# Routed experts after a spectral mixing layer: the first expert product turned round, in tiles of 512, 256 and 128 rows

## The chip, the core and the metric

One core of a Trainium2 chip runs the kernel. The metric is the device time of one execution in microseconds (us); the median of three runs of the kernel before is 2474.87 us. The profile is one further look at an execution: its span runs from the first to the last instruction. [...]

## The reference, cut to what matters

```python
# x: (8, 2496, 256), all float32
X = np.fft.rfft(x, axis=1)
y = np.fft.irfft(X * (filt_r + 1j * filt_i)[None], n=2496, axis=1)
x = y.reshape(19968, 256)                       # N = 19968 tokens of D = 256
logits = x @ w_gate                             # E = 8 experts
expert = argmax(logits, 1)
gate = softmax(logits)[range(N), expert]
for e in range(8):                              # F = 1024
    rows = (expert == e)
    out[rows] = gate[rows, None] * (np.maximum(x[rows] @ w1[e], 0) @ w2[e])
```

Every token goes to one expert, and none is dropped, so how many rows an expert has is known only on the chip.

## The kernel before, in words

The kernel has two stages. The **transform** takes the eight batches through four small matrix stages (`stage_a`, `stage_bc`, `stage_d`) that overlap from batch to batch and pass their data through DRAM (`zd`, `ud`, `yd`). After each batch `route` finds each token's expert and gate, and scatters (token, gate) into a `table` in DRAM with 26 indirect DMAs from GpSimd (POOL), L368. Expert e's tokens stand in the table from row e*N on. The order of the instructions in this stage is worked out by a planner from its own estimates of their times. The planner also places the eight 1 MB loads of w1 (L391), which stay on the chip in `w1s`, the eight loads of w2 (L438), and the short VectorE program (L405 to L428) that finds for each tile its expert and its first row in the table.

The **expert stage** treats 163 tiles of 128 rows of one expert each. Its order is written out by hand (L511 to L522). For one tile:

- `gather` (L442): SP reads the tile's first row from `rrow` into a register and loads 128 table rows (`idt`, L445); POOL gathers the tokens' rows of `yd` (`xg`, L453). The first of the table loads waits for all scatters.
- `turn_x` (L458): two TensorE transposes of 128x128 bring x into `xT`, with its 256 columns on the partitions, through one PSUM bank and a copy.
- `hidden` (L468): x is stationary, and w1 streams through. Two PSUM banks of 128 rows x 512 hidden columns take two products each; in float32 every product is issued as two instructions. ScalarE and VectorE apply the relu.
- `turn_h` (L483): eight transposes turn h, four to a bank, with a copy by each of ScalarE and VectorE.
- `result` (L495): eight products of 256 columns with the turned h as the stationary side and w2 streaming; ScalarE applies the gates; POOL scatters the rows into the output (L502).

In one step of the loop the gather of tile i, the transposes of x of tile i-3, the transposes of h of tile i-5, the hidden product of tile i-4 and the result of tile i-5 are issued in this order. Each engine runs its own instructions in order, and SP's loads share one DMA queue.

Of the kernel before, what the change touches and what calls it, by code (L numbers as in the profile page):

```python
# [105 lines left out]
    # of P = X*Fr and Q = X*Fi, with Yr = Pr - Qi and Yi = Pi + Qr  # L106
# [13 lines left out]
def kernel(  # L120
# [18 lines left out]
    NT = (N + E * (P - 1)) // P  # L139
    TR = E * N + (NT - N // P + 1) * P  # L140
# [6 lines left out]
    # Expert e's tokens, in any order, from row e*N on: (token, gate); unused rows hold token N.  # L147
# [4 lines left out]
    w1s = perm.tile([P, E, DH, F], F32, name="w1s")  # L152
# [166 lines left out]
    def route(b, lgr):  # L319
# [33 lines left out]
        # row = e*N + count before this batch + in this batch's earlier t + in this t's earlier q  # L353
# [13 lines left out]
        for t in range(N2):  # L367
# [6 lines left out]
            # Every token has a row of its own: the scatters need no order among themselves.  # L374
# [24 lines left out]
    erow = tt.tile([1, NT], I32, name="erow")  # L399
    rrow = tt.tile([1, NT], I32, name="rrow")  # L400
    c_i = tt.tile([1, E], I32, name="c_i")
    nt = tt.tile([1, E], F32, name="nt")
    end = tt.tile([1, E], F32, name="end")
# [142 lines left out]
```

## Time and profile before

| | |
|---|---|
| time, three runs | 2455.88, 2474.87, 2485.93 us |
| median | 2474.87 us |
| span of the profiled execution | 2287.2 us |
| instructions | 25424 |
| PE busy / weight loads (PEld) | 88% / 57% |
| DVE, ACT, POOL busy | 25%, 18%, 23% |
| mean granted clock | 0.917 |
| moved by DMA | 191.90 MB, mean 84 GB/s |

The profiled execution has no time of its own beside its span; the median lies 187.7 us above the span. PE is TensorE's products and transposes, PEld its weight loads, which can run under products. In the timeline a row may merge several instructions of a kind: the row's start is that of the first, its length goes to the end of the last, and x8 is their number. Rows of the DMA-issuing queues (SPq) show when a transfer was issued and not when it landed. [...]

### The profile page before, as it was taken

What the parts mean: (1) busy time and instruction counts of PE and PEld (TensorE: products, weight loads), DVE (VectorE), ACT (ScalarE), POOL (GpSimd) and SP (SyncE); (2) the same over time, 40 slices, a digit from 0 to 9 for tenths busy, and PEclk for the clock granted to TensorE, in tenths of its full rate; (3) what the DMA queues carried; (4) which work ended last, traced back from release to release, by engine and by line L of the source; (5) the groups of instructions that cost most, each with busy time, mean ns of one, the idle gap of its engine ahead of it and who ended that gap; (6) DMA issues with size and microseconds to landing.
All of it is one profiled execution on the core that took longest, in us unless ns stands there. A gap on an engine that the chain in (4) does not pass through costs nothing. (4 is left out here: it accounts for less than half of the span.)

```text
span 2287.2 us, 25424 instructions
## 1 busy us (share of the span) xinstructions
PE 2006.8 (88%) x8246; PEld 1303.9 (57%) x8246; DVE 562.6 (25%) x911; ACT 417.6 (18%) x750; POOL 519.0 (23%) x550
## 2 busy tenths in 40 slices
PE   0468888888888888099999999999999999999998
PEld 0224444444444446066667776667777667777666
DVE  0122323232323233222222222222222222222221
ACT  0112111111211112012222222222222222222221
POOL 0000122130404042622222222222222222222221
PEclk9898779877977788599999999999999999999999
DMA  8875556563837354611111111111111111111110
GB/s 145 231 222 164 135 155 150 144 158 111 185 113 177 112 128 122 154 32 33 34 36 33 32 33 33 34 36 33 32 33 33 33 35 32 33 33 33 35 34 15
DMA packets 127074, 191.90 MB, mean 84 GB/s; under 512 B 41687, under 2 KB 93603, under 8 KB 126596
## 3 DMA queue, kind: packets, MB, share of 16 engines
q1 hardware_dynamic: 104648, 148.28, 25.9%
q0 software_dynamic: 22304, 42.01, 5.8%
q8 instruction: 75, 1.23, 0.2%
q14 instruction: 47, 0.39, 0.1%
HBM read 104.42 MB, written 84.15 MB: 82 GB/s over the span
## 5 line engine op out<-in xcount | busy, mean ns | idle before, releaser
L475 PE MATMUL hps<-w1s,xT 128*128 x1304 | 589.7, 595 | 1.0 <-DMA idt<-table 0.9
L499 PE MATMUL yps<-w2s,hT 128*128 x2608 | 589.6, 379 | 0.3 <-ACT hT L493 0.3
L499 PEld LDWEIGHTS yps<-w2s,hT 128*128 128x128 f32 x2608 | 495.4, 190 | 137.0 <-issue 77.0
L502 POOL DMA_INDIRECT out_dram<-ys,idt x163 | 165.7, 1016 | 933.4 <-ACT ys L501 933.4
L475 PEld LDWEIGHTS hps<-w1s,xT 128*128 128x128 f32 x1304 | 236.1, 191 | 237.2 <-issue 235.9
L368 POOL DMA_INDIRECT table<-pay,row x208 | 193.1, 928 | 766.5 <-DVE row L365 430.4
L281 PE MATMUL bank<-pq,tcs 104*104 104x512 f32 x352 | 226.6, 778 | 84.1 <-DVE pq L270 84.1
L479 DVE TENSOR_SCALAR h<-hps 128x512 f32<-128x512 f32 x163 | 112.8, 692 | 452.6 <-PE hps L475 452.6
L501 ACT ACTIVATE ys<-yps,idt 128x256 f32<-128x256 f32 x163 | 77.4, 475 | 736.3 <-PE yps L499 736.3
L464 DVE COPY xT<-pt 128x256 f32<-128x256 f32 x163 | 69.2, 425 | 505.7 <-PE pt L462 468.0
L270 DVE TENSOR_TENSOR pq<-bank,ht 104x1024 f32<-104x1024 f32 x96 | 117.6, 1225 | 268.6 <-PE bank L266 253.2
L253 PE MATMUL bank<-xt,tas 96*96 96x512 f32 x208 | 119.3, 706 | 65.5 <-DMA xt<-in_x_dram 65.5
L453 POOL DMA_INDIRECT xg<-yd,idt x163 | 158.2, 971 | 60.2 <-issue 53.0
L489 PE MATMUL pt<-ident,h 128*128 128x128 f32 x1304 | 169.2, 273 | 0.1
L281 PEld LDWEIGHTS bank<-pq,tcs 104*104 104x104 f32 x352 | 63.7, 203 | 176.8 <-DVE pq L270 113.5
L481 ACT ACTIVATE h<-hps 128x512 f32<-128x512 f32 x163 | 97.3, 597 | 317.1 <-PE hps L475 317.1
L266 PE MATMUL bank<-zi,tbs 104*104 104x256 f32 x384 | 133.7, 473 | 22.8 <-DMA zi<-zd 22.8
L282 ACT COPY uo<-bank 104x512 f32<-104x512 f32 x96 | 56.3, 586 | 501.5 <-PE bank L281 395.8
L489 PEld LDWEIGHTS pt<-ident,h 128*128 128x128 f32 x1304 | 147.5, 141 | 0.6 <-DVE h L479 0.4
L491 DVE COPY hT<-pt 128x512 f32<-128x512 f32 x163 | 112.8, 692 | 88.1 <-PE pt L489 88.1
L266 PEld LDWEIGHTS bank<-zi,tbs 104*104 104x104 f32 x384 | 78.9, 218 | 77.8 <-issue 60.8
L253 PEld LDWEIGHTS bank<-xt,tas 96*96 96x96 f32 x208 | 40.5, 198 | 136.0 <-issue 66.2
(76 smaller groups left out, 961.2 us busy)
## 6 DMA issues: line engine op xcount, KB each, us to landing
zi<-zd SPq DMA_DIRECT2D x48, 416.0 KB
ud<-uo SPq DMA_DIRECT2D x48, 416.0 KB
xt<-in_x_dram SPq DMA_DIRECT2D x48, 384.0 KB
zd<-zo SPq DMA_DIRECT2D x48, 384.0 KB
ui<-ud SPq DMA_DIRECT2D x48, 384.0 KB
yd<-yo SPq DMA_DIRECT2D x48, 384.0 KB
w1s<-in_moe_w_dram SPq DMA_DIRECT2D x8, 1024.0 KB
w2s<-in_moe_w_dram SPq DMA_DIRECT2D x8, 1024.0 KB
```

The costliest lines, as they stand in the source:

```text
L253: mm(ps[:N1, :], lhsT=tas, rhs=xt[:, j:j + 2, :], start=True, stop=True)
L266: mm(ps[:K2, i * D:(i + 1) * D], lhsT=tbs[:, p0 + j + i, :], rhs=zi[:, j + i, :], start=True, stop=True)
L270: nc.vector.tensor_mul(pq, z2[:, None].to_broadcast((K2, 2, 2, D)), ht[:, :, p0 + j:p0 + j + 2, :])
L281: mm(ps[:K2, :], lhsT=tcs[:, s, :], rhs=pq[:, s], start=(s == 0), stop=(s == 1))
L368: sc = nc.gpsimd.indirect_dma_start(out=table, out_offset=bass.IndirectOffsetOnAxis(ap=row[:, t:t + 1], axis=0), in_=pay[:, t, :], in_offs ...
L453: nc.gpsimd.indirect_dma_start(out=xg, out_offset=None, in_=yd, in_offset=bass.IndirectOffsetOnAxis(ap=idt[i].bitcast(U32)[:, 0:1], axis=0))
L475: mm(ps, lhsT=xT[:, dh, :], rhs=w1s[:, bass.ds(ev, 1), dh, fh * 512:(fh + 1) * 512], start=(dh == 0), stop=(dh == DH - 1))
L479: nc.vector.tensor_scalar_max(o, ps, 0.0)
L489: nc.tensor.transpose(pt[:, j, :], h[:, (k + j) * P:(k + j + 1) * P], ident)
L491: nc.vector.tensor_copy(hs[i][:, k:k + 4, :], pt)
L499: mm(ps, lhsT=hT[:, ft, :], rhs=w2s[:, bass.ds(ev, 1), ft, :], start=(ft == 0), stop=(ft == FT - 1))
L502: nc.gpsimd.indirect_dma_start(out=out, out_offset=bass.IndirectOffsetOnAxis(ap=idt.pop(i).bitcast(U32)[:, 0:1], axis=0), in_=ys, in_offse ...
```

## The change

w1 is no longer kept on the chip. Each tile copies its expert's w1 (1 MB) into one of four buffers `w1t` by a load on SP's queue. In `hidden` a 128x128 block of w1 is the stationary side and the turned x streams, so that h comes out with its hidden columns on the partitions; `turn_h` is gone. Eight PSUM banks per tile are filled one after the other, each by two products of as many columns as the tile has rows. A tile has 512, 256 or 128 rows: 31 of 512 are taken from the experts' full blocks, then 8 of 256, and then 23 of 128; `tile_map` runs three times to find their experts and rows. A tile of 512 rows has one table load, four gathers, and four results of 128 rows each, with four scatters. The copies out of PSUM go to VectorE and ScalarE in turn. In the hand-written order the w2 loads are issued after tile 0's table load and w1 copy; within a step the order is gather and w1 copy of tile i+3, hidden of tile i, transposes of x of tile i+1, result of tile i-1.

```diff
@@ the rows of a tile, the table's size, w1's buffer @@
-    NT = (N + E * (P - 1)) // P
-    TR = E * N + (NT - N // P + 1) * P
+    TILES, left = [], N
+    for rows in (512, 256):
+        n = (left - E * (rows - 1)) // rows
+        TILES.append((rows, n))
+        left -= rows * n
+    TILES.append((P, (left + E * (P - 1)) // P))
+    TR = E * N + (E + 1) * P
-    w1s = perm.tile([P, E, DH, F], F32, name="w1s")
@@ the experts @@
     run_all(a0)
...
-            nc.sync.dma_start(out=w1s[:, e], in_=moe_w1[e].rearrange("(i p) f -> p i f", p=P))
         run_all(*([stage_bc(b)] if b < B else []), *([stage_a(b + 1)] if b + 1 < B else []),
...
     tt = ctx.enter_context(tc.tile_pool(name="tt", bufs=1))
...
+    done = tt.tile([1, E], F32, name="done")
+    nc.vector.memset(done, 0.0)
...
+    def tile_map(rows, n, last):
+        av_i = tt.tile([1, E], I32, name="av_i")
+        av = tt.tile([1, E], F32, name="av")
+        end = tt.tile([1, E], F32, name="end")
+        nc.vector.tensor_tensor(av, cnt[0:1, :], done, op=ALU.subtract)
+        nc.vector.tensor_scalar(av_i, in0=av, scalar1=float(rows - 1 if last else 0), scalar2=None, op0=ALU.add)
+        nc.vector.tensor_scalar(
+            av_i, in0=av_i, scalar1=rows.bit_length() - 1, scalar2=None, op0=ALU.arith_shift_right
+        )
+        nc.vector.tensor_copy(av, av_i)
+        nc.vector.tensor_tensor_scan(end, one, av, 0.0, op0=ALU.mult, op1=ALU.add)
+        base = tt.tile([1, E], F32, name="base")
+        add = tt.tile([1, E], F32, name="add")
+        nc.vector.tensor_tensor(base, done, eoff[0:1, :], op=ALU.add)
+        nc.vector.tensor_scalar(add, in0=av, scalar1=-float(rows), scalar2=None, op0=ALU.mult)
+        nc.vector.tensor_tensor(add, add, base, op=ALU.subtract)
+        nc.vector.tensor_tensor(add[:, :E - 1], add[:, :E - 1], base[:, 1:], op=ALU.add)
+        tau_i = tt.tile([1, n], I32, name="tau_i")
+        tau = tt.tile([1, n], F32, name="tau")
+        nc.gpsimd.iota(tau_i, pattern=[[1, n]], base=0, channel_multiplier=0)
+        nc.vector.tensor_copy(tau, tau_i)
+        past = tt.tile([1, n, E - 1], F32, name="past")
+        she = (1, n, E - 1)
+        nc.vector.tensor_tensor(
+            past, tau[:, :, None].to_broadcast(she), end[:, None, :E - 1].to_broadcast(she), op=ALU.is_ge
+        )
+        ef = tt.tile([1, n], F32, name="ef")
+        erow = tt.tile([1, n], I32, tag=f"erow{rows}", name="erow")
+        nc.vector.tensor_reduce(ef, past, axis=AX.X, op=ALU.add)
+        nc.vector.tensor_copy(erow, ef)
+        nc.vector.tensor_tensor(past, past, add[:, None, :E - 1].to_broadcast(she), op=ALU.mult)
+        rf = tt.tile([1, n], F32, name="rf")
+        rrow = tt.tile([1, n], I32, tag=f"rrow{rows}", name="rrow")
+        nc.vector.tensor_reduce(rf, past, axis=AX.X, op=ALU.add)
+        nc.vector.tensor_scalar(tau, in0=tau, scalar1=float(rows), scalar2=base[:, 0:1], op0=ALU.mult, op1=ALU.add)
+        nc.vector.tensor_tensor(rrow, rf, tau, op=ALU.add)
+        if not last:
+            take = tt.tile([1, E], F32, name="take")
+            nc.vector.tensor_tensor(take, av, end, op=ALU.subtract)
+            nc.vector.tensor_scalar(take, in0=take, scalar1=float(n), scalar2=0.0, op0=ALU.add, op1=ALU.max)
+            nc.vector.tensor_tensor(take, take, av, op=ALU.min)
+            nc.vector.tensor_scalar(take, in0=take, scalar1=float(rows), scalar2=None, op0=ALU.mult)
+            nc.vector.tensor_tensor(done, done, take, op=ALU.add)
+        return [(rows // P, erow[0:1, i:i + 1], rrow[0:1, i:i + 1]) for i in range(n)]
+    work = []
+    for k, (rows, n) in enumerate(TILES):
+        work += tile_map(rows, n, k == len(TILES) - 1)
     w2p = ctx.enter_context(tc.tile_pool(name="w2p", bufs=1))
     moe = ctx.enter_context(tc.tile_pool(name="moe", bufs=3))
     psh = ctx.enter_context(tc.tile_pool(name="psh", bufs=3, space=PSUM))
-    psx = ctx.enter_context(tc.tile_pool(name="psx", bufs=3, space=PSUM))
+    psx = ctx.enter_context(tc.tile_pool(name="psx", bufs=2, space=PSUM))
     psy = ctx.enter_context(tc.tile_pool(name="psy", bufs=2, space=PSUM))
...
-        nc.sync.dma_start(out=w2s[:, e], in_=moe_w2[e].rearrange("(i p) d -> p i d", p=P))
...
+    flip = [0]
+    def either(on_vector, on_scalar):
+        flip[0] += 1
+        (on_vector if flip[0] % 2 else on_scalar)()
+    idt, xgs, xts, w1t, hs = {}, {}, {}, {}, {}
     def gather(i):
-        r0 = nc.sync.value_load(rrow[0:1, i:i + 1], min_val=0, max_val=TR - P)
-        idt[i] = moe.tile([P, 2], I32, tag="idt", name="idt", bufs=8)
-        ld = nc.sync.dma_start(out=idt[i], in_=table[bass.ds(r0, P), :])
+        n, e, r = work[i]
+        r0 = nc.sync.value_load(r, min_val=0, max_val=TR - n * P)
+        idt[i] = moe.tile([P, 4, 2], I32, tag="idt", name="idt", bufs=8)
+        ld = nc.sync.dma_start(
+            out=idt[i][:, :n], in_=table[bass.ds(r0, n * P), :].rearrange("(p i) c -> p i c", i=n)
+        )
         if i == 0:
             for name in scatters:
                 tc.add_manual_dep(
                     ld.ins, name, mybir.DependencyInfo(mybir.DependencyClass.Sync, mybir.DependencyReason.DATA),
                     reason="all of the table is written",
                 )
-        xg = moe.tile([P, D], F32, tag="xg", name="xg", bufs=5)
-        nc.gpsimd.indirect_dma_start(
-            out=xg, out_offset=None, in_=yd, in_offset=bass.IndirectOffsetOnAxis(ap=idt[i].bitcast(U32)[:, 0:1], axis=0)
-        )
-        xts[i] = xg
+        xgs[i] = moe.tile([P, 4, D], F32, tag="xg", name="xg", bufs=5)
+        for j in range(n):
+            nc.gpsimd.indirect_dma_start(
+                out=xgs[i][:, j], out_offset=None, in_=yd,
+                in_offset=bass.IndirectOffsetOnAxis(ap=idt[i].bitcast(U32)[:, j, 0:1], axis=0),
+            )
+    def weights(i):
+        ev = nc.sync.value_load(work[i][1], min_val=0, max_val=E - 1)
+        w1t[i] = moe.tile([P, DH, F], F32, tag="w1t", name="w1t", bufs=4)
+        nc.sync.dma_start(out=w1t[i], in_=moe_w1[bass.ds(ev, 1)].rearrange("o (i p) f -> p (o i) f", p=P))
     def turn_x(i):
-        xg = xts[i]
-        pt = psx.tile([P, 4, P], F32, tag="pt", name="pt")
+        n, xg = work[i][0], xgs.pop(i)
+        xts[i] = moe.tile([P, DH, 4 * P], F32, tag="xT", name="xT", bufs=2)
         for dh in range(DH):
-            nc.tensor.transpose(pt[:, dh, :], xg[:, dh * P:(dh + 1) * P], ident)
-        xts[i] = moe.tile([P, DH, P], F32, tag="xT", name="xT")
-        nc.vector.tensor_copy(xts[i], pt[:, :DH, :])
-
-    evs = {}
+            pt = psx.tile([P, 4, P], F32, tag="pt", name="pt")
+            for j in range(n):
+                nc.tensor.transpose(pt[:, j, :], xg[:, j, dh * P:(dh + 1) * P], ident)
+            o = xts[i][:, dh, :n * P].rearrange("p (j q) -> p j q", j=n)
+            either(lambda: nc.vector.tensor_copy(o, pt[:, :n]), lambda: nc.scalar.copy(out=o, in_=pt[:, :n]))
     def hidden(i):
-        ev = evs[i] = nc.tensor.value_load(erow[0:1, i:i + 1], min_val=0, max_val=E - 1)
-        xT = xts.pop(i)
-        hs[i] = moe.tile([P, F], F32, tag="h", name="h")
-        for fh in range(2):
+        m = work[i][0] * P
+        xT, w1 = xts.pop(i), w1t.pop(i)
+        hs[i] = []
+        for k in range(FT):
             ps = psh.tile([P, 512], F32, tag="h", name="hps")
             for dh in range(DH):
-                mm(ps, lhsT=xT[:, dh, :], rhs=w1s[:, bass.ds(ev, 1), dh, fh * 512:(fh + 1) * 512],
+                mm(ps[:, :m], lhsT=w1[:, dh, k * P:(k + 1) * P], rhs=xT[:, dh, :m],
                    start=(dh == 0), stop=(dh == DH - 1))
-            o = hs[i][:, fh * 512:(fh + 1) * 512]
-            if fh:
-                nc.vector.tensor_scalar_max(o, ps, 0.0)
-            else:
-                nc.scalar.activation(o, ps, AF.Relu)
-
-    def turn_h(i):
-        h = hs[i]
-        hs[i] = moe.tile([P, FT, P], F32, tag="hT", name="hT")
-        for k in range(0, FT, 4):
-            pt = psx.tile([P, 4, P], F32, tag="pt", name="pt")
-            for j in range(4):
-                nc.tensor.transpose(pt[:, j, :], h[:, (k + j) * P:(k + j + 1) * P], ident)
-            if k:
-                nc.vector.tensor_copy(hs[i][:, k:k + 4, :], pt)
-            else:
-                nc.scalar.copy(out=hs[i][:, k:k + 4, :], in_=pt)
+            hT = moe.tile([P, 512], F32, tag="hT", name="hT", bufs=2 * FT)
+            either(lambda: nc.vector.tensor_scalar_max(hT[:, :m], ps[:, :m], 0.0),
+                   lambda: nc.scalar.activation(hT[:, :m], ps[:, :m], AF.Relu))
+            hs[i].append(hT)
     def result(i):
-        ev, hT = evs.pop(i), hs.pop(i)
-        ps = psy.tile([P, D], F32, tag="y", name="yps")
-        for ft in range(FT):
-            mm(ps, lhsT=hT[:, ft, :], rhs=w2s[:, bass.ds(ev, 1), ft, :], start=(ft == 0), stop=(ft == FT - 1))
-        ys = moe.tile([P, D], F32, tag="ys", name="ys", bufs=4)
-        nc.scalar.activation(ys, ps, AF.Copy, scale=idt[i].bitcast(F32)[:, 1:2])
-        nc.gpsimd.indirect_dma_start(
-            out=out,
-            out_offset=bass.IndirectOffsetOnAxis(ap=idt.pop(i).bitcast(U32)[:, 0:1], axis=0),
-            in_=ys,
-            in_offset=None,
-            bounds_check=N - 1,
-            oob_is_err=False,
-        )
-
+        n, e, r = work[i]
+        ev = nc.tensor.value_load(e, min_val=0, max_val=E - 1)
+        hT, ids = hs.pop(i), idt.pop(i)
+        for j in range(n):
+            ps = psy.tile([P, D], F32, tag="y", name="yps")
+            for k in range(FT):
+                mm(ps, lhsT=hT[k][:, j * P:(j + 1) * P], rhs=w2s[:, bass.ds(ev, 1), k, :],
+                   start=(k == 0), stop=(k == FT - 1))
+            ys = moe.tile([P, D], F32, tag="ys", name="ys", bufs=6)
+            gate = ids.bitcast(F32)[:, j, 1:2]
+            either(lambda: nc.vector.tensor_scalar(ys, in0=ps, scalar1=gate, scalar2=None, op0=ALU.mult),
+                   lambda: nc.scalar.activation(ys, ps, AF.Copy, scale=gate))
+            nc.gpsimd.indirect_dma_start(
+                out=out,
+                out_offset=bass.IndirectOffsetOnAxis(ap=ids.bitcast(U32)[:, j, 0:1], axis=0),
+                in_=ys,
+                in_offset=None,
+                bounds_check=N - 1,
+                oob_is_err=False,
+            )
+    n = len(work)
     with tc.manual_schedule():
-        for i in range(NT + 5):
-            if i < NT:
-                gather(i)
-            if 3 <= i < NT + 3:
-                turn_x(i - 3)
-            if 5 <= i:
-                turn_h(i - 5)
-            if 4 <= i < NT + 4:
-                hidden(i - 4)
-            if 5 <= i:
-                result(i - 5)
+        for i in range(-3, n + 1):
+            if 0 <= i + 3 < n:
+                gather(i + 3)
+                weights(i + 3)
+                if i + 3 == 0:
+                    for e in range(E):
+                        nc.sync.dma_start(out=w2s[:, e], in_=moe_w2[e].rearrange("(i p) d -> p i d", p=P))
+            if i == -1:
+                turn_x(0)
+            if 0 <= i < n:
+                hidden(i)
+            if 0 <= i and i + 1 < n:
+                turn_x(i + 1)
+            if 1 <= i:
+                result(i - 1)
```

## Rows read from the trace of the kernel before

**Rows 1.** Page, totals by engine: busy us, share of the span, instructions.
```profile
PE 2006.8 (88%) x8246; PEld 1303.9 (57%) x8246; DVE 562.6 (25%) x911; ACT 417.6 (18%) x750; POOL 519.0 (23%) x550
```

**Rows 2.** Stretches: length, busy time by engine, then PE clock, DMA share, GB/s.
```profile
600.00:850.00 250.00, 212.29 (x814) 117.56 (x813) 75.57 (x112) 42.01 (x76) 64.53 (x71) 0.80 0.58 140
...
1000.00:1300.00 300.00, 300.00 (x1282) 211.16 (x1281) 67.66 (x113) 61.62 (x112) 73.57 (x74) 1.00 0.11 33
```

**Rows 3.** Timeline, TensorE, one tile of the expert stage: start, length, instructions.
```profile
1500.15 3.60 PE L475 MATMUL hps<-w1s,xT 128*128 x8
1503.58 3.62 PE L499 MATMUL yps<-w2s,hT 128*128 x16
1507.04 0.38 PE L462 MATMUL pt<-ident,xg 128*128 128x128 f32 x2
1507.26 1.04 PE L489 MATMUL pt<-ident,h 128*128 128x128 f32 x8
1508.13 2.31 PE L475 MATMUL hps<-w1s,xT 128*128 x5
```

**Rows 4.** Groups by line, weight loads: busy us, mean ns of one | idle before.
```profile
L499 PEld LDWEIGHTS yps<-w2s,hT 128*128 128x128 f32 x2608 | 495.4, 190 | 137.0 <-issue 77.0 <-ACT hT L493 0.5 <-ACT h L481 0.5
L475 PEld LDWEIGHTS hps<-w1s,xT 128*128 128x128 f32 x1304 | 236.1, 191 | 237.2 <-issue 235.9 <-DVE xT L464 1.3
...
L489 PEld LDWEIGHTS pt<-ident,h 128*128 128x128 f32 x1304 | 147.5, 141 | 0.6 <-DVE h L479 0.4
...
L310 PEld LDWEIGHTS lg<-wg,yt 128*96 128x96 f32 x832 | 82.9, 167 | 28.6 <-ACT yt L186 18.9 <-DVE yt L188 6.1
```

**Rows 5.** Groups by line, copies of 512 columns out of PSUM.
```profile
L491 DVE COPY hT<-pt 128x512 f32<-128x512 f32 x163 | 112.8, 692 | 88.1 <-PE pt L489 88.1
...
L493 ACT COPY hT<-pt 128x512 f32<-128x512 f32 x163 | 95.5, 586 | 39.0 <-DVE xT L464 35.8 <-PE pt L489 3.2
```

**Rows 6.** Timeline, all engines, from the transform's end to the first product.
```profile
919.15 26.43 SPq L438 DMA_DIRECT2D w2s<-in_moe_w_dram  x8
...
964.27 27.94 SPq L445 DMA_DIRECT2D idt<-table  x9
967.42 0.98 POOL L453 DMA_INDIRECT xg<-yd,idt  x1 [5.17 <-DMA idt<-table]
968.71 0.96 POOL L453 DMA_INDIRECT xg<-yd,idt  x1 [0.30 <-issue]
...
970.61 0.66 PE L462 MATMUL pt<-ident,xg 128*128 128x128 f32 x2 [52.14 <-DMA xg<-yd,idt]
...
973.04 6.64 PE L475 MATMUL hps<-w1s,xT 128*128 x8 [0.86 <-DMA idt<-table]
```

**Rows 7.** Timeline, POOL, the last batch's 26 scatters: first, two of 25 steps, last.
```profile
927.37 1.76 POOL L368 DMA_INDIRECT table<-pay,row  x1 [2.04 <-DVE row L365]
...
933.55 0.92 POOL L368 DMA_INDIRECT table<-pay,row  x1 [0.30 <-issue]
934.78 0.92 POOL L368 DMA_INDIRECT table<-pay,row  x1 [0.30 <-issue]
...
961.33 0.92 POOL L368 DMA_INDIRECT table<-pay,row  x1 [0.30 <-issue]
```

**Rows 8.** Stretches, columns as in rows 2, while the w2 loads are under way.
```profile
920.00:930.00 10.00, 0.00 (x0) 0.00 (x0) 4.70 (x13) 0.00 (x0) 6.43 (x8) 0.50 1.02 230
...
950.00:960.00 10.00, 0.00 (x0) 0.00 (x0) 0.00 (x0) 0.00 (x0) 6.51 (x8) 0.50 0.60 139
```

**Rows 9.** Timeline, all engines, the first loads of the transform's second stage.
```profile
82.53 1.86 SPq L391 DMA_DIRECT2D w1s<-in_moe_w_dram  x1
88.10 0.32 SPq L261 DMA_DIRECT2D zi<-zd  x1
...
94.68 2.01 PE L266 MATMUL bank<-zi,tbs 104*104 104x256 f32 x4 [13.20 <-DMA zi<-zd]
```

**Rows 10.** Timeline, all engines, TensorE's last work.
```profile
2274.30 3.72 PE L499 MATMUL yps<-w2s,hT 128*128 x16 [0.28 <-ACT hT L493]
```

More of the change, by code (lines that the diff above doesn't have):

```diff
@@ L389 @@
     for b in range(B + 1):
-        for e in range(b * E // (B + 1), (b + 1) * E // (B + 1)):
-            nc.sync.dma_start(out=w1s[:, e], in_=moe_w1[e].rearrange("(i p) f -> p i f", p=P))
         run_all(*([stage_bc(b)] if b < B else []), *([stage_a(b + 1)] if b + 1 < B else []),
@@ L397 @@
     tt = ctx.enter_context(tc.tile_pool(name="tt", bufs=1))
[L399 to L403, printed above, removed]
+    done = tt.tile([1, E], F32, name="done")
+    nc.vector.memset(done, 0.0)
     one = tt.tile([1, E], F32, name="one")
-    nc.vector.tensor_scalar(c_i, in0=cnt[0:1, :], scalar1=float(P - 1), scalar2=None, op0=ALU.add)
@@ L406 @@
-    nc.vector.tensor_scalar(c_i, in0=c_i, scalar1=7, scalar2=None, op0=ALU.arith_shift_right)
-    nc.vector.tensor_copy(nt, c_i)
     nc.vector.memset(one, 1.0)
-    nc.vector.tensor_tensor_scan(end, one, nt, 0.0, op0=ALU.mult, op1=ALU.add)
-    tau_i = tt.tile([1, NT], I32, name="tau_i")
-    tau = tt.tile([1, NT], F32, name="tau")
-    nc.gpsimd.iota(tau_i, pattern=[[1, NT]], base=0, channel_multiplier=0)
-    nc.vector.tensor_copy(tau, tau_i)
-    past = tt.tile([1, NT, E - 1], F32, name="past")
@@ L415 @@
-    she = (1, NT, E - 1)
-    nc.vector.tensor_tensor(
-        past, tau[:, :, None].to_broadcast(she), end[:, None, :E - 1].to_broadcast(she), op=ALU.is_ge
-    )
-    ef = tt.tile([1, NT], F32, name="ef")
-    nc.vector.tensor_reduce(ef, past, axis=AX.X, op=ALU.add)
-    nc.vector.tensor_copy(erow, ef)
-    nc.vector.tensor_tensor(past, past, nt[:, None, :E - 1].to_broadcast(she), op=ALU.mult)
-    st = tt.tile([1, NT], F32, name="st")
-    nc.vector.tensor_reduce(st, past, axis=AX.X, op=ALU.add)
@@ L425 @@
-    nc.vector.tensor_tensor(st, tau, st, op=ALU.subtract)
-    nc.vector.tensor_scalar(st, in0=st, scalar1=float(P), scalar2=None, op0=ALU.mult)
-    nc.vector.tensor_scalar(ef, in0=ef, scalar1=float(N), scalar2=None, op0=ALU.mult)
-    nc.vector.tensor_tensor(rrow, st, ef, op=ALU.add)
+    def tile_map(rows, n, last):
[42 more added lines that the diff above has]
+        return [(rows // P, erow[0:1, i:i + 1], rrow[0:1, i:i + 1]) for i in range(n)]
@@ L433 @@
     psh = ctx.enter_context(tc.tile_pool(name="psh", bufs=3, space=PSUM))
-    psx = ctx.enter_context(tc.tile_pool(name="psx", bufs=3, space=PSUM))
+    psx = ctx.enter_context(tc.tile_pool(name="psx", bufs=2, space=PSUM))
     psy = ctx.enter_context(tc.tile_pool(name="psy", bufs=2, space=PSUM))
     w2s = w2p.tile([P, E, FT, D], F32, name="w2s")
-    for e in range(E):
-        nc.sync.dma_start(out=w2s[:, e], in_=moe_w2[e].rearrange("(i p) d -> p i d", p=P))
-    idt, xts, hs = {}, {}, {}
-    def gather(i):
-        r0 = nc.sync.value_load(rrow[0:1, i:i + 1], min_val=0, max_val=TR - P)
-        idt[i] = moe.tile([P, 2], I32, tag="idt", name="idt", bufs=8)
-        ld = nc.sync.dma_start(out=idt[i], in_=table[bass.ds(r0, P), :])
+    flip = [0]
[3 more added lines that the diff above has]
+    idt, xgs, xts, w1t, hs = {}, {}, {}, {}, {}
+    def gather(i):
+        n, e, r = work[i]
[4 more added lines that the diff above has]
+        )
         if i == 0:
```

1 line of the change is left out of this document (removed).

## The prediction

> **What bounds the kernel now.** I read first the totals by engine, then the table by stretches, then one tile of the expert stage in time order. TensorE holds 88% of the span [rows 1], but the share is a mean over two stages. [...] One tile of 128 rows [rows 3] lasts from 1500.15 to 1508.13, 7.98 us: the hidden product (8 instructions) runs to 1503.58, 3.43 us; the result (16) to 1507.04, 3.46; x's two transposes to 1507.26, 0.22; the eight transposes of h to 1508.13, 0.87. These starts, not the printed lengths, are the price, since the instructions overlap. Per instruction: 512 columns 0.429 us, 256 columns 0.216, a transpose 0.109. Columns set it: 0.84 ns each. 163 tiles of 7.98 us are 1300.7 us; TensorE's last work ends at 2274.30 + 3.72 = 2278.0 [rows 10], so a stage without a slow start would have begun at 977.3.
>
> **The sum's base.** The page gives a span of 2287.2 us. The median of three runs is 2474.87, so 187.7 us lie around the span; I keep them as they are. A change of span is taken as the same change of time.
>
> **Part 1, the transposes of h.** 163 x 0.87 = **-142 us**, all on the path. Their two copies out of PSUM (0.69 us on VectorE, a like one on ScalarE) go too, but those were covered.
>
> **Part 2, the hidden product turned round.** A block of 512 rows needs 8 x 2 products of 512 columns, each two instructions: 32 x 0.429 = 13.7 us, just four times 3.43. For 256 rows 32 x 0.216 is the same per row. Tiles are 31 of 512, 8 of 256, 23 of 128 rows, again 163 blocks of 128, so the result and x's transposes are unchanged. Only the 128-column instructions have no row. There are 23 x 32 = 736. Lower bound: columns, 0.429 / 4 = 0.107 us, no loss. The weight load may be longer. Four rows [rows 4] give busy time per load: 0.190 (495.4 / 2608) and 0.181 where loads stand apart, 0.113 for transposes' loads, 0.0996 (82.9 / 832) where 96-column loads follow each other behind eight-column products. The last is nearest, since there the load alone sets the pace; by columns 128 make 0.133. Cost 736 x 0.026 = **+19 us**; upper bound, loads of 0.190 that do not overlap each other, +61.
>
> The trace shows loads under products: 512-column products follow at their columns' pace though each has a load of 0.19 us in it [rows 3, 4].
>
> [...]
>
> **Part 3, the copies of w1.** Before, eight loads of 1 MB during the transform; after, 62, one per tile. For 512 rows a tile lasts 4 x 7.11 = 28.4 us, for 128 rows 7.1. The w2 loads moved at 230 GB/s with the DMA engines full [rows 8], so 1.05 MB take 4.6 us, under 7.1. On SP the load for tile i+3 waits until hidden(i-1) has let its buffer go, and the table read of tile i+4 is queued behind it; POOL's gathers for i+4 wait for that read and stand ahead of tile i's scatters. Read, gather and landing need about 4.6 + 3.2 + 3.2 us [rows 6, 8] of some 28 before turn_x(i+4). Cost 0; if that cover is gone, see the third rival.
>
> **Part 4, copies out and waits.** Per 512 rows the h copies fall from 16 to 8, each 0.69 us or less [rows 5], beside 13.7 us of products and three banks. x's copy (0.69 for 512 columns) lies beside result(i-1), 3.4 us at least. Value loads on TensorE fall from 163 to 62, none visible now [rows 2]. POOL issues as many gathers and scatters as before. Cost 0.
>
> **Part 5, the start of the expert stage.** Here I expect a new wait. Before, the eight w2 loads were issued at 919.15, beside the last batch's scatters, and the first table read at 964.27, after the last scatter; gathers at 967.42, 1.27 us apart, the first product at 973.04 [rows 6]. After, w2 is issued behind tile 0's table read and w1 copy, and tile 1's read, copy and gathers are behind w2 on the same SP queue.
> The 26 scatters ran 927.37 to 961.33; at their 1.23 us step 25 steps are 30.7 us, so about 3 us were lost beside w2 [rows 7]. These return; three tile maps in place of one on VectorE may cost 0 to 8 us ahead of the last scatters, though only the first is needed at once; I take +1.5. Tile 0's read: 962.5.
> w2 took 919.15 to about 956 (DMA share 1.02 falling to 0.60 in 950 to 960 [rows 8]), 37 us for 8.4 MB; with w1's first copy 41.6. Tile 1's read lands at 962.5 + 1 + 41.6 + 2 = 1007, its fourth gather at 1007 + 0.5 + 3 x 1.27 + 3.2 = 1014.5, and hidden(1) starts at 1016.5 (second transpose to product was 1.5 to 2 us). hidden(0) starts near 977 and is done by 994, so TensorE stands about 20 us; the DMA queue is what is late. [...] Left are 163 x 7.11 - 13.7 - 1.8 = 1143.4 us, so without part 2's 19 the end is 2162.9, and a stage without a slow start would have begun at 2162.9 - 1158.9 = 1004.0, not 977.3: **+27 us**. Bounds: +12, where the read lands as soon as SP has issued w2 (26.4 us, [rows 6]); +40, where tile 0's gathers are held up by w2 too and the maps cost 8.
>
> **Part 6, the transform without w1.** The second of the eight w1 loads is issued at 82.53, ahead of the first zi load at 88.10, whose product runs at 94.68 [rows 9]. A load of 1 MB is 4.6 us by part 3, and the zd writes that zi waits for pass beside the first; I take **-5.5** in all. Bounds: -12, the whole gap, and +15, since the transform's order is planned anew without these loads and nothing shows that it comes out better.
>
> Sum: -142 + 19 + 27 - 5.5 = -101.5. Span 2186, **time 2373 us**, 4.1% less.
>
> **Rivals.**
> 1. *Loads of 0.190 us set the small tiles.* For: that is the busy time of a load in this stage. Against: 96-column loads went by in 0.0996. +42 on the sum: 2415. Chance 0.12.
> 2. *No wait at the start.* For: another queue's packets mix in; against: SP itself took 26.4 us to issue w2. With +12 in place of +27 and loads hidden (-19): 2339. Chance 0.12.
> 3. *The w1 copies set the pace of the 23 small tiles.* For: the transform with its smaller pieces moved only 140 GB/s at a share of 0.58 [rows 2], so 240 at full, and beside it run gathers and scatters. Against: 230 here. At a copy of 8 us, 23 x 0.9 = +21: 2394. Chance 0.09.
> 4. *Load and 128-column product add up.* Place: the 23 small tiles. 0.190 + 0.107 = 0.297 us, 736 x 0.190 = +140 in place of 19: 2373 + 121 = 2494, slower than before. It decides from 0.107 + 120.5 / 736 = 0.271 us on. For: no row has a 128-column f32 product. Against: the transposes, 128 columns each, pass in 0.109 with a load each [rows 3, 4]. Chance 0.04.
> 5. *The transform comes out differently* by 15 us or more: 2388 to 2440. Chance 0.07, a third of it over 2425.
>
> The forecast itself has 0.53, with 2345 to 2400 as its own range. What no row shows has 0.03. That the transposes stay is no rival: no call is left.
>
> **Numbers.** About 2% (49 us) is what a measurement here tells from no change; the runs shown differ by 30. Low end: rival 2 with the whole gap of part 6 and half the runs' scatter, 2339 - 6.5 - 15 = 2318. High end: rival 1 and the rest of part 5's bound, 2415 + 13 = 2428. Left out are rival 4, the upper ends of rivals 1 and 5 (0.07), 0.04 below and the 0.03 of no named case. Within 2%: 0.03 of rival 4, 0.05 of rival 1 (with another loss beside it) and 0.02 of rival 5, 0.10. Slower by over 2% (above 2524): rival 4 with part 5's upper bound, 0.01, and 0.03 for what no row shows, 0.04. Faster by over 2% (under 2425): the rest, 0.86.
>
> **What would show it.** Part 1: no transposes of h, and hidden at 13.7 us per 512 rows. Part 2: starts of 128-column products 0.133 us apart. Part 3: no TensorE gap between small tiles and DMA share under 1. Part 5: about 20 us of idle between hidden(0) and turn_x(1), ended by a gather, at clock 0.50 before hidden(1). Part 6: the first zi product some 5 us earlier. Wrong would be: TensorE gaps in steady tiles, a clock under 1.00 there, or a transform that moves by more than 15 us.

## The result and the profile after

The median is 2350.28 us (2329.2 to 2357.7, four runs), beside it before 2465.38 us (2454.81 to 2485.93, four runs): **ratio 0.951, 95% interval 0.944 to 0.958**. The forecast was 2373 us, range 2318 to 2428. Ratios leave out executions over 1.5% above the fastest of their kernel, so some differ a little from the quotient of the medians.

The totals by engine on the page of after, to be held against [rows 1]: TensorE has 624 instructions fewer (7622 for 8246).

```profile
span 2342.1 us, 22213 instructions
...
PE 1904.0 (81%) x7622; PEld 1261.6 (54%) x7622; DVE 465.6 (20%) x862; ACT 323.7 (14%) x652; POOL 512.7 (22%) x552
```

That span is 55 us longer than that of before's page, 2287.2, and yet after is faster. In every profiled run whose own time is on record the time is the span plus 1.7 us (2343.8 for this one). If that holds for the page of before too, it was an execution some 176 us shorter than the timed runs beside it, and no work lies around the span. Where these 176 us are can be read from one more profile of before, e1 below: its **expert stage**, from the first read of the table (SP's `idt` load) to the end of the span, lasts 2469.6 - 1146.69 = 1322.9 us, and in before's page 2287.2 - 964.27 = 1322.9 as well. All the rest is in the transform. So I split every run at that read and count what lies ahead of it as the transform.

| kernel | median us | span | first read | expert stage | ratio to before (95%) |
|---|---|---|---|---|---|
| before, its page | | 2287.2 | 964.27 | 1322.9 | |
| e1, before again | 2471.33 (one) | 2469.6 | 1146.69 | 1322.9 | |
| after | 2350.28 | 2342.1 | 1138.48 | 1203.6 | 0.951 (0.944 to 0.958) |
| e2 w2 first | 2343.45 | 2338.5 | 1146.19 | 1192.3 | 0.952 (0.943 to 0.962) |
| e3 before, h not turned | 2310.56 | 2298.5 | 1119.27 | 1179.2 | 0.942 (0.933 to 0.950) |
| e4 w1 loads back in the transform | 2367.05 | 2374.1 | 1169.96 | 1204.1 | 0.960 (0.953 to 0.967) |
| e13 = e7, scatters spread | 2274.86 | 2274.5 | 1071.50 | 1203.0 | **0.917** (0.910 to 0.924) |
| e5 tiles of 128 only | 2207.66 | 2207.7 | 970.64 | 1237.1 | 0.963 (0.952 to 0.974) |
| e7 scatters spread | 2171.55 | 2150.6 | 947.18 | 1203.4 | 0.953 (0.944 to 0.961) |
| e8 spread and w2 first | 2169.48 | 2143.4 | 954.15 | 1189.3 | 0.952 (0.943 to 0.960) |
| e9 before, spread | 2300.52 | 2292.2 | 969.06 | 1323.1 | 1.007 (1.002 to 1.012) |
| e10 after again | 2167.97 | 2174.0 | 970.46 | 1203.5 | 0.947 (0.941 to 0.954) |
| e11 = e7 | 2167.29 | 2168.5 | 965.40 | 1203.1 | 0.946 (0.937 to 0.954) |
| e12 = e8 | 2169.45 | 2157.5 | 968.45 | 1189.1 | 0.952 (0.943 to 0.960) |

Beside after and e1 to e4 and e13 the kernel before takes 2465 to 2480 us; beside e5 and e7 to e12 it takes 2288 to 2292. Only ratios and expert stages go across these two groups.

The expert stage of after, TensorE in time order, to be held against [rows 3]; first a tile of 512 rows, then one of 128.

```profile
1199.77 13.98 PE L531 MATMUL yps<-w2s,hT 128*128 x64
1213.59 13.90 PE L517 MATMUL hps<-xT,w1t 128*128 128x512 f32 x32
1227.32 1.04 PE L506 MATMUL pt<-ident,xg 128*128 128x128 f32 x8
1228.19 13.98 PE L531 MATMUL yps<-w2s,hT 128*128 x64
...
2249.02 3.73 PE L517 MATMUL hps<-xT,w1t 128*128 128x128 f32 x32
2252.59 0.38 PE L506 MATMUL pt<-ident,xg 128*128 128x128 f32 x2
2252.81 3.67 PE L531 MATMUL yps<-w2s,hT 128*128 x16
2256.32 3.73 PE L517 MATMUL hps<-xT,w1t 128*128 128x128 f32 x32
```

A tile of 512 rows lasts 28.42 us, 7.105 per 128; no transposes of h are left. The 32 products of 128 columns take 2252.59 - 2249.02 = 3.57 us, 0.112 each; over 21 such tiles, from 2168.82 to 2322.07, a tile lasts 7.30 us. Two stretches (columns as in rows 2), the second all of small tiles, show TensorE busy throughout at clock 1.00 (the granted clock, as a share of full speed), with the DMA engines at a share of 0.50 at most:

```profile
1300.00:1800.00 500.00, 500.00 (x1822) 333.45 (x1821) 78.67 (x124) 69.70 (x124) 138.12 (x141) 1.00 0.23 75
2180.00:2320.00 140.00, 140.00 (x958) 131.35 (x957) 31.64 (x106) 30.23 (x106) 35.84 (x36) 1.00 0.50 159
```

The groups by line and form, to be held against [rows 4, 5]: a load of w1 takes 191 ns, as the loads did before, and stands under products; a copy out takes 692 ns beside its 1.7 us of products (4 x 0.43).

```profile
L517 PEld LDWEIGHTS hps<-xT,w1t 128*128 128x128 f32 x1984 | 324.2, 191 | 234.8 <-issue 224.7 <-ACT xT L508 0.5 <-DVE xT L508 0.3
...
L520 DVE TENSOR_SCALAR hT<-hps 128x512 f32<-128x512 f32 x124 | 85.8, 692 | 398.9 <-PE hps L517 389.5 <-issue 9.4
```

The start of the expert stage, SP, POOL and TensorE in time order, to be held against [rows 6]:

```profile
1138.48 0.38 SPq L479 DMA_DIRECT2D idt<-table  x1
...
1140.13 22.45 SPq L554 DMA_DIRECT2D w2s<-in_moe_w_dram  x8
...
1152.99 15.74 PE L517 MATMUL hps<-xT,w1t 128*128 128x512 f32 x32
1163.37 2.18 SPq L479 DMA_DIRECT2D idt<-table  x1
1172.07 0.95 POOL L490 DMA_INDIRECT xg<-yd,idt  x1 [25.84 <-DMA idt<-table]
...
1178.07 0.45 PE L506 MATMUL pt<-ident,xg 128*128 128x128 f32 x1 [9.34 <-DMA xg<-yd,idt]
...
1182.96 16.10 PE L517 MATMUL hps<-xT,w1t 128*128 128x512 f32 x32
```

TensorE has finished hidden(0) and stands 9.34 us for tile 1's gather; POOL stood 25.84 us for tile 1's table read, which was issued behind w2. hidden(1) starts 44.5 us after the first read.

### The profile page after: what moved, and what is told of

It is laid out like the page before. It is cut to its first block, busy times and chain, and to the rows that moved or that the text cites. A ratio compares the mean times of both kernels' runs of the same rounds, so it can differ in the third digit from the quotient of the medians.

```text
span 2342.1 us, 22213 instructions
## 1 busy us (share of the span) xinstructions
PE 1904.0 (81%) x7622; PEld 1261.6 (54%) x7622; DVE 465.6 (20%) x862; ACT 323.7 (14%) x652; POOL 512.7 (22%) x552
## 5 line engine op out<-in xcount | busy, mean ns | idle before, releaser
L517 PE MATMUL hps<-xT,w1t 128*128 128x512 f32 (+2 forms) x1984 | 577.3, 449 | 0.0
L531 PE MATMUL yps<-w2s,hT 128*128 x2608 | 574.0, 379 | 0.0
L517 PEld LDWEIGHTS hps<-xT,w1t 128*128 128x128 f32 x1984 | 324.2, 191 | 234.8 <-issue 224.7
L520 DVE TENSOR_SCALAR hT<-hps 128x512 f32<-128x512 f32 (+2 forms) x248 | 126.2, 509 | 551.9 <-PE hps L517 539.4
L315 PE MATMUL lg<-wg,yt 128*96 128x8 f32 x832 | 97.8, 244 | 128.3 <-ACT yt L191 62.7
L521 ACT ACTIVATE hT<-hps 128x512 f32<-128x512 f32 (+2 forms) x248 | 111.9, 451 | 489.4 <-PE hps L517 444.9
L315 PEld LDWEIGHTS lg<-wg,yt 128*96 128x96 f32 x832 | 94.7, 189 | 147.9 <-ACT yt L191 70.7
L535 DVE TENSOR_SCALAR ys<-yps,idt 128x256 f32<-128x256 f32 x82 | 39.6, 483 | 364.3 <-PE yps L531 364.3
L301 PE MATMUL bank<-ui,tds 96*96 96x256 f32 x416 | 110.3, 404 | 2.0 <-DMA ui<-ud 2.0
L536 ACT ACTIVATE ys<-yps,idt 128x256 f32<-128x256 f32 x81 | 38.4, 474 | 486.6 <-PE yps L531 486.6
```

The lines of the kernel that those rows point to most:

```text
L315: mm(lg[:, 0, t * E:(t + 1) * E], lhsT=yt[:, 2 * i + dh, :], rhs=wg[:, dh, :], start=(dh == 0), stop=(dh == DH - 1))
L517: mm(ps[:, :m], lhsT=w1[:, dh, k * P:(k + 1) * P], rhs=xT[:, dh, :m], start=(dh == 0), stop=(dh == DH - 1))
L520: either(lambda: nc.vector.tensor_scalar_max(hT[:, :m], ps[:, :m], 0.0), lambda: nc.scalar.activation(hT[:, :m], ps[:, :m], AF.Relu))
L521: lambda: nc.scalar.activation(hT[:, :m], ps[:, :m], AF.Relu))
L531: mm(ps, lhsT=hT[k][:, j * P:(j + 1) * P], rhs=w2s[:, bass.ds(ev, 1), k, :], start=(k == 0), stop=(k == FT - 1))
```

## The experiments

Each kernel but e1, which is before, is timed beside before; "first read" and "expert stage" are columns of the table above.

**e1, before again**, no edit, to see the execution that the timed runs have.

> The kernel before, one more look. The runs of the changed kernel last 1.7 us longer than their spans, so the 187.7 us between the profiled span of before (2287.2) and its median cannot lie around the span. Theory: the profiled execution of before had a shorter transform than its timed runs. This run then has a span of about 2463 us, the first table read near 1140 and not 964, and an expert stage of 1323 us from there to the end as before. Rival: the time lies around the span, which is 2287 again with the first read near 964.

Measured: 2471.33 us, span 2469.6, the expert stage equal to 0.1 us: the time does not lie around the span, as the theory had it. What differs in the transform is seen in one stretch of 50 us (columns as in rows 2) around the first batch's 26 scatters: before's page, e1, after, and then e10, beside which before takes 2292 us.

```profile
270.00:320.00 50.00, 43.49 (x143) 22.78 (x143) 15.16 (x21) 7.66 (x14) 24.10 (x26) 0.74 0.69 158
```
```profile
270.00:320.00 50.00, 22.48 (x93) 14.65 (x92) 12.50 (x28) 3.67 (x7) 24.03 (x26) 0.64 0.55 125
```
```profile
270.00:320.00 50.00, 25.74 (x70) 14.01 (x71) 9.72 (x21) 3.13 (x6) 23.90 (x26) 0.57 0.44 104
```
```profile
270.00:320.00 50.00, 44.18 (x156) 23.34 (x156) 13.53 (x15) 8.14 (x15) 22.09 (x25) 0.77 0.62 154
```

POOL scatters alike in all four; TensorE does 43 to 44 us of work in two of them and 22 to 26 in the others. After's timeline of POOL, TensorE and ScalarE in that stretch shows what it waits for:

```profile
278.14 1.07 POOL L373 DMA_INDIRECT table<-pay,row  x1 [275.81 <-DMA zi<-zd]
...
294.15 0.84 PE L315 MATMUL lg<-wg,yt 128*96 128x8 f32 x8 [1.09 <-issue]
294.86 0.53 PE L307 MATMUL pt<-ident,yo 96*128 96x96 f32 x4
...
308.74 0.92 POOL L373 DMA_INDIRECT table<-pay,row  x1 [0.31 <-issue]
...
314.00 0.48 ACT L191 COPY yt<-pt 128x384 f32<-128x384 f32 x1 [19.89 <-remote]
314.53 1.45 PE L315 MATMUL lg<-wg,yt 128*96 128x8 f32 x8 [19.15 <-ACT yt L191]
```

The four transposes end at 295.39, and the copy of their bank, on ScalarE, which does nothing else from 294.10 on, starts at 314.00: 18.6 us late, 4.3 us after the last of the 26 scatters has ended. I measured this lag for all 104 copies of `yt` in each trace, from the end of the transposes (or the engine's last work) to the copy's start. In after 14 copies are over 1 us late, 137.6 us together; in e1 14, 135.1 us; in e2 to e4 12 to 14; in before's page and in e10 none, the largest lag being 0.11 us. All the late ones start within a run of back-to-back scatters or up to 6 us behind it. I call these executions ones with **late copies**.

**e3, before without the turning** (left out: h enters the result's products as it is).

```diff
-        h = hs[i]
-        hs[i] = moe.tile([P, FT, P], F32, tag="hT", name="hT")
-        for k in range(0, FT, 4):
...
+        hs[i] = hs[i].rearrange("p (k q) -> p k q", k=FT)
```

> The kernel before without the transposes of h and their copies: the unturned h is used as the stationary side, so the numbers of the output are not the reference's. Theory (the transposes are all on TensorE's path): 163 x 0.87 = 142 us less, a tile of 7.11 us, 2323 us, ratio 0.942. Rival (without them TensorE waits for the relu copies of h or for the tokens): a tile longer than 7.11 us and gaps of TensorE inside it, ratio above 0.96.

Measured: 2310.56 us, 0.942. The expert stage is 143.7 us shorter; TensorE is busy in all of 1170 to 2280 us, and a tile lasts 7.11 us:

```profile
1500.59 3.62 PE L490 MATMUL yps<-w2s,h 128*128 x16
1504.05 0.38 PE L462 MATMUL pt<-ident,xg 128*128 128x128 f32 x2
1504.26 3.60 PE L475 MATMUL hps<-w1s,xT 128*128 x8
1507.70 3.62 PE L490 MATMUL yps<-w2s,h 128*128 x16
```

So the transposes, with their copies, were all on the path, and the change gives back 143.7 - 119.3 = 24.4 us of them elsewhere.

**e5, tiles of 128 rows only**: 163 copies of w1 and 5216 products of 128 columns in place of 62 and 736.

```diff
-    for rows in (512, 256):
+    for rows in ():
```

> The kernel after with 163 tiles of 128 rows only, so w1 is copied 163 times (171 MB in place of 65) and every product of hidden has 128 columns: 163 x 32 = 5216 instructions in place of 736. Theory (what the trace of after showed at its small tiles: 0.1116 us per instruction, 7.29 us per tile, loads of weights under products, no gap): the products after tile 1 are 4480 x 0.0044 = 20 us more, and the expert stage lasts about 20 to 25 us longer than after's 1203.6; time about 2375, ratio to before 0.962. The start may be a little shorter, since the first gathers are 1 each and not 4. If the prediction's 0.133 us per instruction were right: 4480 x 0.026 = 116 us more, 2466, ratio 1.00. If the copies of w1 set the pace (1 MB in more than 7.29 us beside gathers and scatters): gaps on TensorE between tiles that end on a DMA; at 8 us per tile 163 x 0.7 = 114 us more, 2464.

Measured: 0.963; the expert stage is 1237.1 us, 33.5 more than after's. The steady tiles of TensorE, and a stretch of them:

```profile
1501.83 3.73 PE L517 MATMUL hps<-xT,w1t 128*128 128x128 f32 x32
1505.40 0.38 PE L506 MATMUL pt<-ident,xg 128*128 128x128 f32 x2
1505.62 3.67 PE L531 MATMUL yps<-w2s,hT 128*128 x16
1509.13 3.73 PE L517 MATMUL hps<-xT,w1t 128*128 128x128 f32 x32
```
```profile
1100.00:1500.00 400.00, 400.00 (x2747) 376.23 (x2747) 92.77 (x302) 86.78 (x303) 109.14 (x110) 1.00 0.56 180
```

7.29 us per tile, 0.112 per product, and TensorE is busy all of the time: neither the loads of weights nor the copies of w1 (1.05 MB in 7.29 us, the DMA engines at 0.56) set the pace. 163 x 7.29 is 25 us above after's 1163 (worked out below). Of the other 8, 10 are that only 3.6 us of work, not 13.8, lie ready for TensorE before it stands for tile 1, and another -5 that hidden(1) starts 39.3 us after the first read, not 44.5; 3 stay unexplained. The prediction's 0.133 us per product would have given 116 us. A load that did not overlap its product would have given 5216 x 0.19, about 990 us.

**e2, w2 first**: the loads of w2 are issued as soon as their buffer is free, not behind tile 0's read.

```diff
+    for e in range(E):      # right behind the allocation of w2s
+        nc.sync.dma_start(out=w2s[:, e], in_=moe_w2[e].rearrange("(i p) d -> p i d", p=P))
...
-                if i + 3 == 0:
-                    for e in range(E): ...
```

> The changed kernel with the eight w2 loads issued ahead of tile 0's table read, as in the kernel before. Theory (the start is late because tile 1's read stands behind w2 on SP's queue): hidden(1) follows hidden(0) with no stand of TensorE for a gather, the scatters lose about 3 us beside w2, and the time falls by about 17 us to 2333, ratio to before 0.946. Rival (the gathers themselves set the start): TensorE still stands some 9 us ahead of tile 1's transposes and the time stays at 2350.

Measured: 2343.45 us, 0.952, not told apart from after; the expert stage is 11.3 us shorter. The stand for tile 1's gather is gone, so the rival falls; but POOL now issues 20 gathers back to back, from 1149.18 to 1173.94, and behind them copies of h are late, by up to 6.2 us. ScalarE and TensorE in time order:

```profile
1160.97 11.95 PE L519 MATMUL hps<-xT,w1t 128*128 128x512 f32 x24
1175.33 0.60 ACT L523 ACTIVATE hT<-hps 128x512 f32<-128x512 f32 x1 [8.65 <-remote]
1175.98 1.98 PE L519 MATMUL hps<-xT,w1t 128*128 128x512 f32 x4 [3.06 <-issue]
```

e8 and e12, without late copies, gain 14.2 and 14.4 us in this stage beside e10. Of the 20 us that the start costs (below), then, 11 (e2) go with w2's place in the queue; e8 and e12 also have fewer buffers of gathered rows, so what each of the two gave of their 14 is not shown.

**e4, the w1 loads back in the transform** (read by nobody; the experts still copy w1 per tile).

```diff
+    w1s = cst.tile([P, E, DH, F], F32, name="w1s")
...
+        for e in range(b * E // (B + 1), (b + 1) * E // (B + 1)):
+            nc.sync.dma_start(out=w1s[:, e], in_=moe_w1[e].rearrange("(i p) f -> p i f", p=P))
```

> The changed kernel with the eight w1 loads put back into the transform, into a buffer that nobody reads. Theory (they delay only the first zi loads): the first product of the second stage comes 5.5 us later (bounds 0 and 12), the rest is unchanged: 2356 us, ratio to before 0.953. Rival (the planner's order without these loads is what made or cost time): the transform differs by 15 us or more from the changed kernel's, in either direction.

Measured: 2367.05 us, 0.960, 16.8 us above after's median, with intervals that overlap. By the medians the transform is 16.3 us longer, over the 15 us of the rival; the overlap leaves it open. The first product on `zi`, after and then e4, stands where the prediction put it, 3.7 us later with the loads:

```profile
89.93 2.01 PE L271 MATMUL bank<-zi,tbs 104*104 104x256 f32 x4 [8.40 <-DMA zi<-zd]
```
```profile
93.61 2.01 PE L272 MATMUL bank<-zi,tbs 104*104 104x256 f32 x4 [12.13 <-DMA zi<-zd]
```

**e7, e8 and e9, the scatters spread**, in after, in after with w2 first and three buffers of gathered rows, and in before: each batch's 26 scatters are issued in the next batch's steps, the first of every four behind the latest copy out of PSUM.

```diff
+            if after and t % 4 == 0:
+                tc.add_manual_dep(sc.ins, mark[0], ...)     # the latest copy out of PSUM
+            if after and t % 4 == 3:
+                yield
...
-                *([stage_d(b - 1)] if b else []))
+                *([stage_d(b - 1)] if b else []), *([scatter(True)] if todo else []))
+    run_all(scatter(False))
```

> The kernel after with the 26 scatters of each batch issued four at a time in the steps of the next batch, each fourth one behind the latest copy out of PSUM, in place of 26 back to back; the last batch's stay together. Theory: the long runs of back-to-back scatters on POOL are what delays the hand-over from TensorE to the copies (5 to 24 us a time, some 12 to 28 us per batch) in the transform, so seven batches get 12 to 25 us shorter each: 85 to 175 us less, time 2175 to 2265, ratio to before 0.88 to 0.92, and no copy in the transform lags TensorE by over 2 us except in the last burst. Rival A: the delay goes with the number of scatters, however they are spaced: then the same lag is split over more places and the time stays at 2350, ratio 0.953. Rival B: the scatters are only beside the delay and the order of the planner is its cause: no change, or some us to either side.

> e7 with the w2 loads issued ahead of the wait for the table (as in e2) and the buffers of gathered rows cut from 5 to 3. Three buffers hold POOL's gathers back to three tiles ahead, so the run of gathers at the start of the expert stage is 12 in place of 20. If the two changes add: e7 less 11 us for w2 first and 0 to 5 us for the shorter run of gathers. By the theory 2160 to 2250; by the rivals about 2336.

> The kernel before with the scatters spread as in e7. Expert stage as before, 1322.9 us. Theory: the transform loses the same 85 to 175 us as e7's, and a run of before gets near the profile's span of 2287: 2290 to 2380, ratio 0.93 to 0.965. Rivals A and B: 2465, ratio 1.00. If e7 and e9 gain the same, the gain of the change (115 us) stands beside it unchanged.

Measured: 0.953, 0.952 and 1.007. These runs could not decide whether the scatters set off the late copies: before itself took 2288.27 us beside them, and no copy is late in e5 either, whose scatters come 26 at a time as in after. Where nothing is late, spreading gains nothing; in before it costs 12 us. e8's shorter expert stage does not show in its time: its transform is 2169.48 - 1.7 - 1189.3 = 978.5 us by the median, e7's 966.4, and the pair of e12 and e11 repeats it (978.7 and 962.5). Why, I leave open; w2 first is no gain in the time. The run of gathers at the start is 16 long in e8, not the 12 that I expected.

**e10 and e11, after and e7 side by side**, and **e12 and e13**, e8 and e7 once more.

> The kernel after once more, unchanged. The four runs of the last study ran on another chip than those ahead of them: the kernel before took 2288.27 us there (13 runs) and 2469.63 on the earlier one. Theory: the expert stage is the same on either chip (1203.6 us from the first read of the table), and the transform alone differs: on a chip where before takes 2288, after takes 2288 - 119 + 5 = 2174, ratio 0.950, and no copy of yt lags TensorE by over 0.2 us; on one where it takes 2470, after takes 2350, ratio 0.952, with lags of 5 to 24 us. Rival: what the change is worth depends on the chip (the w1 copies or the clock): a ratio outside 0.944 to 0.958.

> e7 once more, the scatters spread four at a time, beside the kernel after on the same chip. On a chip where before takes about 2470: theory (runs of back-to-back scatters set off the late copies there) 85 to 175 us less than after's, 2175 to 2265; rival A (the number of scatters counts, not their spacing) and rival B (the scatters are not the cause) both 2350 within 20. On a chip where before takes about 2288 there is nothing to gain, as e7 showed beside before (0.9527): then within 15 us of after's, and the question stays open.

> e8 once more (scatters spread, w2 first, three buffers of gathered rows), beside before. Three chips have run so far: before takes 2470 us on one and 2288 and 2292 on the others. On one of the latter: the expert stage is 1189 us, 14 less than after's, so about 2155 to 2170, ratio 0.942 to 0.952. On one where before takes 2470: theory (back-to-back scatters set off the late copies) 2155 to 2250; rivals A and B (their number, or another cause) 2336 within 20.

> e7 a third time (scatters spread, nothing else changed), for the question that only a chip with late copies can settle, beside before. Where before takes 2470 us: theory (back-to-back scatters set off the late copies) 2175 to 2265, ratio 0.88 to 0.92; rivals (their number, or another cause) 2350 within 20, ratio 0.953. Where before takes about 2290: 2155 to 2185, ratio 0.942 to 0.955, and the question stays open.

Measured: e10 2167.97 us, 0.947 (forecast 2174, 0.950), no late copy: the ratios with and without them can't be told apart. e11 and e12 again ran without late copies and decide nothing. **e13 ran with them**: before 2480.11 us, e7 2274.86, ratio 0.917 beside after's 0.951. The intervals lie apart, and both rivals had 0.953. So the late copies come with long runs of scatters: the same number of scatters in shorter runs delays them less, and e7 is the fastest of the kernels that ran where copies are late, and equal to after where they are not (2167.29 and 2167.97 us). The edit also changes the planner's order, which is worth nothing by itself where no copy is late; the length of the runs alone was not varied. The first read comes 67 us earlier than in after, the expert stage is the same; the copies over 1 us late are 13 and sum to 74.9 us in place of 137.6. The gain is under the 85 to 175 us that I expected, and POOL's timeline shows a reason: the edit spread less than I meant.

```profile
279.90 1.07 POOL L379 DMA_INDIRECT table<-pay,row  x1 [277.57 <-DMA zi<-zd]
281.27 0.91 POOL L379 DMA_INDIRECT table<-pay,row  x1 [0.31 <-issue]
...
301.93 0.91 POOL L379 DMA_INDIRECT table<-pay,row  x1 [0.30 <-issue]
307.57 0.91 POOL L379 DMA_INDIRECT table<-pay,row  x1 [4.73 <-ACT yt L193]
323.83 0.91 POOL L379 DMA_INDIRECT table<-pay,row  x1 [15.35 <-ACT yt L193]
337.07 0.91 POOL L379 DMA_INDIRECT table<-pay,row  x1 [12.33 <-ACT yt L193]
```

19 scatters still go back to back, until 302.84, and seven follow one by one. ScalarE's copies are late behind the 19 (the second by 8.6 us, at 306.81, 4.0 after the run's end) and on time beside the single ones. The run starts 1.8 us later than after's (279.90 for 278.14) and ends 6.8 us sooner (302.84 for 309.66), and the copy behind it starts 7.2 us sooner (306.81 for 314.00):

```profile
295.49 0.48 ACT L193 COPY yt<-pt 128x384 f32<-128x384 f32 x1 [6.54 <-remote]
306.81 0.48 ACT L193 COPY yt<-pt 128x384 f32<-128x384 f32 x1 [10.85 <-remote]
...
321.21 0.48 ACT L193 COPY yt<-pt 128x384 f32<-128x384 f32 x1 [1.72 <-PE pt L309]
323.07 0.48 ACT L193 COPY yt<-pt 128x384 f32<-128x384 f32 x1 [1.38 <-PE pt L309]
```

## Why the prediction was right, step by step

The mechanism held: the transposes' time came back, less a little for the small tiles and the start. The two smaller terms of the expert stage were oversized. The stage came out at -119.3 us where the steps gave -96 (parts 1, 2, 4 and 5): -143.7, +4.0 and +20.4 in place of -142, +19 and +27 (the last is what the other two leave).

- **The sum's base was misread.** "187.7 us lie around the span" is wrong: 1.7 do, and the rest was a longer transform, whose late copies (135 us in e1) the profiled execution did not have. It cost the forecast nothing, since both kernels carry them alike (137.6 us in after; ratios 0.951 and 0.947). That was luck: no row of before shows a late copy.
- **Part 1**, -142: e3 measured -143.7. That TensorE is what the stage of before waits on, [rows 2] show (busy 300 of 300 us).
- **Part 2**, +19, was the step that missed. The work after is 31 x 28.42 + 8 x 14.25 (a 256-row tile's step in the timeline) + 23 x 7.30 = 1162.9 us, 4.0 above 163 x 7.11. The small products come at 0.112 us, almost the lower bound by columns (0.107), and e5 has it over 5216 of them. What failed was to scale the 0.0996 us of 96-column loads [rows 4] up by columns to 0.133: loads of 128 columns pass at 0.112, and what set the pace in that row no run shows. The better row stood beside it, the transposes with 128 columns, a load each, at 0.109 [rows 3].
  Load and product do not add up: the 128-row loads of 191 ns pass under 128-column products 112 ns apart, PEld busy for 131.35 of the 140.00 us in which TensorE is. By the pace of 0.112 us rival 4 falls, and rival 1 (0.190) too.
- **Part 3**, 0: right. No gap among small tiles, in e5 not even with 163 copies. Rival 3 falls.
- **Part 4**, 0: right; TensorE is busy in all of the 1130 us between 1200 and 2330.
- **Part 5**, +27: the wait is where it was put, on tile 1's read behind w2, but it cost 20, and the stand is 9.3 us, not 20. The clock did fall, to 0.50 from 1174 to 1187 us, and hidden(1) lasts 16.10 us and not 13.90. No trace of after shows the 3 us that the end at 2162.9 holds beside 1016.5 and 1143.4; it shows these 2.2 in their place. Mis-sized was the rate. I took the 230 GB/s of [rows 8], when the last scatters ran beside w2; after's stretches show 348 (315 from 1140 to 1150):

```profile
1150.00:1160.00 10.00, 8.74 (x19) 4.14 (x20) 1.38 (x2) 1.18 (x2) 0.00 (x0) 0.67 1.10 348
1160.00:1170.00 10.00, 8.73 (x21) 3.60 (x19) 2.07 (x3) 1.79 (x3) 0.00 (x0) 1.00 1.11 349
```

  9.44 MB at 348 GB/s are 27 us and not 41.6, so tile 1's first gather ran 33.6 us after the first read and not 45 (1007 - 962.5). That the 8-byte scatters had slowed [rows 8] is my reading. e2 and e8, where w2 again runs beside the last scatters, agree: 193 to 249 GB/s in the stretches with a DMA share over 0.9, but for one of 328 (e2, 1105 to 1115); no run takes the scatters away alone. Rival 2's +12 is not reached.
- **Part 6**, -5.5: the first `zi` product is at 89.93 for 94.68, as said. By medians less 1.7 and the expert stage, the transform moved by +4.2 us with late copies (1145.0 against 1140.8) and by -5.1 without (e10: 962.8 against 967.9). e4's +16.8 goes the same way as the step. Its size, and whether it reaches the end of the transform, the scatter of the runs leaves open; between before and after rival 5's 15 us are not reached.

From 2373 to 2350.28: -23.3 in the expert stage, -9.5 because before's median fell to 2465.38 with its fourth run, +9.7 in the transform. The last two cancel by chance.

## What to carry to other kernels

Work on TensorE that only reshapes, in a stage where TensorE is busy all of the time, was worth what it lasts (142 us by the rows, 143.7 measured): choose which operand is stationary so that the product comes out in the next product's layout, and pay with copies of weights while the DMA engines have room (a share of 0.11 here before, 0.23 with the copies in tiles of 512 rows, 0.56 in e5). Short products cost next to nothing here: those of 128 columns, with a weight load each, took 4% more per column than those of 512 (0.1116 us for a quarter of 0.429). Before summing against a profile, compare its span with the timed runs: the four of before lay within 31 us of each other, its profile's span was 167.6 us under the fastest of them, and a split by stages said which stage differed.

## What the runs showed of the hardware

- **In after, copies out of PSUM started up to 20.9 us after TensorE's work for them had ended, around runs of back-to-back indirect DMAs on POOL** (the copy of `yt` at 1070.45, its transposes done at 1049.52, the run's last scatter at 1068.74). The lags of one run end with it or up to 6 us behind (314.00 for 309.66 in after, 306.81 for 302.84 in e13). Copies are late behind the gathers at the start of the expert stage too: behind 20 of them copies of h are up to 6.2 us late in e2, behind 16 only 1.0 in after and 3.1 in e4. In after's steady tiles of 512 rows, with one to five indirect DMAs in a row, the copies of h are at most 0.1 us late; in e13 no copy of `yt` is late beside the single scatters. In after the lags sum to 137.6 us; the transform is 182 us longer than in e10 (1145.0 against 962.8), and shorter runs take back 75 us (e13). Where the other 45 of the 182 us lie was not measured.
- It does not belong to a kernel: before took some 2290 or some 2470 us, in all runs that stood side by side alike. Nor does it to a chip, if the number in the records names one chip each time: number 11 had both (2287.87 beside e12, 2480.11 beside e13). What switches it, and whether the signal, the semaphore or the trace's "remote" event is delayed, no run shows.
- Runs of at most four scatters, each with a wait of its own, were not tried.
